# Attention and a rotating mixer: other ranks and a port rule for the opening, softmax sums beside a constant, first sine z's by two products, q and k behind vb

## The chip, the cores and the metric

The kernel runs on one core of a Trainium2 chip. The metric is the device time of one execution in microseconds; the time before is the median of three runs. The engines are called as in the profile: PE (TensorE), DVE (VectorE), ACT (ScalarE), POOL (GpSimd) and SP (SyncE, which issues the DMAs).

## The reference

```python
scores = q @ k.T / sqrt(64)                      # batch 8, heads 8, seq 576, head_dim 64
scores = where(mask, scores, -1e9)               # heads 0-3: last 32 keys; heads 4-7: every 4th of the last 128
attn = exp(scores - max);  attn = attn / (sum(attn) + 1e-9)
x = (attn @ v) as (8, 576, 512)
theta = x @ w_theta                              # 512 x 512
y = w_tok_r @ (x * cos(theta)) + w_tok_i @ (x * sin(theta))   # 576 x 576 each, over the sequence
u = x + y
out = u + relu(u @ w_ch)                         # 512 x 512, fp32 throughout
```

## The kernel before

The kernel works batch by batch, heads in four pairs (`pr`). Every large product is made in fp32 precision from rounded parts: an operand is split in a high part (a cast, on ACT) and a low part (the difference, on POOL), and three matmuls are added up. For the weights this split follows an unpacking: `unpack` clips (DVE, L407), scales (ACT, L409), prepares the second half (L412 on DVE or L415 on ACT) and joins the two (DVE, L417), and `split` makes the parts (ACT L425, POOL L427).

For each batch and pair: the scores `s` (PE, L547), their mask and maximum (DVE, L486, into P and mx), the exponential with the row sum (ACT, L582), the sum's reciprocal (L585 adds 1e-9, L586, both DVE), the normalisation of P (POOL, L588), the transposes pt<-P (DVE, L606) and the product with the values, `o` (PE, L702), which reads the values in two parts, `va` and `vb`. Then, for five row blocks `st` (4 is the short one), theta (`th`, L774 to L781), its sine and cosine (`trig`: K, f and g are scratch), x transposed (`xn`, L865) and its products with them, by_x (DVE, L856). These are the z's: z_0 to z_3 the cosine's, z_4 to z_7 the sine's, zh_8 and zl_8 both of the short block. `zsplit` makes their high part (a DVE cast, L730, in batch 0 for z_4 to z_8, otherwise ACT, L733) and their low part (POOL, L735). Token units `token(b, d, g)` compute y_d_g (PE, L1371), `residual` adds it to x (DVE, L1344) and splits u (ACT L1347, POOL L1349); channel units `chan(b, e, g)` compute c_e_g (PE, L1404), and `finish` does relu and add (DVE, L1380) and so frees their PSUM bank. In batch 0 all units take turns at the two banks "m". xh is x split for theta (L676 to L682).

From batch 2 on the token product is a faster scheme with sums of the token weights. These are built once, in batch 1, from wt_g, late_wt_a and others (POOL, L1069 to L1092), stored to DRAM (tw_t, tw_b; SP, L1098), and fetched in each batch (SP, L1049).

The order of the program on each engine is not written out by hand. The class `Order` runs the tasks as generators: each yields the engine that it wants next and an estimated cost in ns (functions dve, dve2, act, pool and others), or an event that it waits for, and of those ready on the engine that is free first the task of lowest rank goes. In the opening (batches 0 and 1) the ranks are the table RANK; after that `steady()` gives due times instead. What is pinned so is each engine's program order. Each engine, SP with its loads and stores too, works through its own order, and waits on the chip for whatever an instruction needs. Loads of q and k are in `load_qk` (L273, L275), of va and vb in L287 and L304.

Of the kernel before, what the change touches and what calls it, by code (L numbers as in the profile page):

```python
# [32 lines left out]
RANK = dict(load=6.64, scores0=1.09, flip=0.01, pv0=1.13, pair=.21, theta_unpack=1.54, theta0=5.3, trig0=2.41,  # L33
            token_early=2.55, theta_split=6.42, token_late=6.75, chan=2.1, units=2.95, evacuate=4.49,
            scores1=4.02, scores2=7.3, pv1=8.0, theta1=5.96, trig1=7.42)
# [45 lines left out]
class Order:  # L81
# [6 lines left out]
    def __init__(self, tc):  # L88
        self.tc = tc
        self.live = self.steady = False  # L90
        self.now = 0.0
        self.tasks, self.free, self.events = [], {}, {}
        self.serial = 0
        self.func = None

# [7 lines left out]
    def go(self, gen, rank=None):  # L103
# [5 lines left out]
        t = [self.rank if rank is None else rank, self.serial, self.now, gen, None, 0.0, None, False, 0.0]  # L109
# [3 lines left out]
    def advance(self, t):  # L113
        keep = getattr(self, "rank", None)
        self.rank = t[0]
        try:
# [12 lines left out]
            if t[7]:  # L129
                t[4] = "DVE"  # L130
# [6 lines left out]
    def run(self):  # L137
        while any(t[0] < BACK or self.steady for t in self.tasks):
# [7 lines left out]
            else:  # L146
# [9 lines left out]
                end = at + t[5]  # L156
                if eng == "ACT" and t[6]:
# [12 lines left out]
SLACK = 1500.0  # L170
# [15 lines left out]
def pool(n):  # L186
    return 2.36 * n
# [15 lines left out]
def build(ctx, tc, qT, kT, vw, wth, wtk, wch, maskb, ident, identb, outT):  # L203
# [60 lines left out]
    def load_qk(n):  # L264
# [4 lines left out]
        r = yield from take("qk", 2)  # L269
        q = ap.tile([128, 2 * NJ, 2 * QB], F32, tag="q", name=f"q{b}_{pr}")  # L270
# [20 lines left out]
    def load_vb(n):  # L291
# [51 lines left out]
    pqs, pts = [], []  # L343

# [41 lines left out]
    def unpack(src, sz, name, stage, early, n, key):  # L386
# [19 lines left out]
        yield "DVE", dve2(sz)  # L406
        pin(nc.vector.tensor_scalar(C, C, W_MAX, -W_MAX, op0=ALU.min, op1=ALU.max))  # L407
        yield "ACT", act(sz)
        pin(nc.scalar.activation(C, C, AF.Prelu, scale=2.0 ** -112, alpha=-2.0 ** 32))  # L409
        if early and n % 2 == 0:  # L410
            yield "DVE", dve2(sz)
            pin(nc.vector.tensor_scalar(Ti, Ti, 29, None, op0=ALU.logical_shift_right))  # L412
        else:
            yield "ACT", act(sz)
            pin(nc.scalar.activation(Ti, Ti, AF.Copy, scale=2.0 ** -29, bias=-0.5))  # L415
        yield "DVE", dve(sz)
# [101 lines left out]
    def scores(b, pr):  # L518
# [12 lines left out]
        sm = sp.tile([128, NJ], F32, tag=f"sm{b == 0 and pr}", name=f"sm{b}_{pr}", bufs=1 if b == 0 else 2)  # L531
# [39 lines left out]
        if b == 0:  # L571
# [3 lines left out]
            pin(nc.vector.tensor_reduce(sm, P, op=ALU.add, axis=mybir.AxisListType.X))  # L575
        elif not on_pe(b, pr):
            if b == 1:
                yield None, "sin0"
            for n0 in range(0, NJ, 3):
                yield "EXP", 1000 if od.steady else 720  # L580
                for n in range(n0, n0 + 3):
                    table(nc.scalar.activation(P[:, n], P[:, n], AF.Exp, bias=mx[:, n:n + 1], scale=-1.0,  # L582
                                               accum_out=sm[:, n:n + 1]))
        yield "DVE", 200
        pin(nc.vector.tensor_scalar(sm, sm, 1e-9, None, op0=ALU.add))  # L585
# [1073 lines left out]
```

## Time and profile before

| | |
|---|---|
| median of 3 runs | 564.25 us (562.17 to 565.25) |
| profiled execution | 563.72 us, of which the span 562.0 |
| PE busy | 532.8 us, 95% of the span |
| DVE busy | 440.9 us, 78% |
| ACT busy | 377.4 us, 67% |
| POOL busy | 332.4 us, 59% |

The span is the time from the first to the last instruction of the profiled execution; the rest of its 563.72 us lies around it. Busy shares are means over stages that differ: the opening, in which batch 0's attention and the unpacking of the weights share all engines, and the steady batches.

### The profile page before, as it was taken

Reading aid. Unit: us, or ns where it says so; the run is one execution under the profiler, and the core shown is the slowest. Engines: PE = TensorE matmul, PEld = TensorE weight load, DVE = VectorE, ACT = ScalarE, POOL = GpSimd, SP = SyncE. Lnnn points to the kernel's source line nnn. Section 1 sums busy time; section 2 is a strip of 40 time slices with the busy share of each in tenths; the row PEclk is TensorE's granted clock in tenths of the full one; section 3 lists DMA queues with packets and bytes.
Section 4 is the critical chain, followed back from the end, with each engine's and each line's share of the span. In section 5 each row is a group of like instructions: output and inputs, shape, how many; then the busy total and the mean of one; then the engine's idle time right before and its main releaser. Section 6 shows DMA issues by size and latency. Waiting matters only on the chain.

```text
span 562.0 us, 14370 instructions
## 1 busy us (share of the span) xinstructions
PE 532.8 (95%) x5296; PEld 483.3 (86%) x5296; DVE 440.9 (78%) x1347; ACT 377.4 (67%) x1033; POOL 332.4 (59%) x351
## 2 busy tenths in 40 slices
PE   5898798989999999999999999999999999999997
PEld 3644687868998899998999899989999899989997
DVE  3879698985579696999799997999799988838422
ACT  1598978768748577667876677768866777457320
POOL 1328759787994273674567284655468365817660
PEclk9999598989999999999999999999999999999999
DMA  8991436721678859985598919994798727690622
GB/s 299 400 390 28 178 117 217 250 81 65 207 244 276 298 213 310 317 247 202 175 351 275 302 54 338 320 244 152 257 342 235 269 91 235 188 265 24 224 93 86
DMA packets 59127, 124.42 MB, mean 221 GB/s; under 512 B 5424, under 2 KB 24624, under 8 KB 58800
## 3 DMA queue, kind: packets, MB, share of 16 engines
q1 hardware_dynamic: 59056, 123.49, 65.2%
q8 instruction: 42, 0.69, 0.5%
q14 instruction: 29, 0.24, 0.1%
HBM read 99.88 MB, written 23.59 MB: 220 GB/s over the span
## 4 chain that ended last, share of the span: by engine, by line
PE 58%; DVE 15%; POOL 8%; ACT 8%; DMA 7%; issue 3%; SPq 1%; POOLq 0%; DVEq 0%; ACTq 0%
PE c L1404 14%; PE th L774 11%; PE C L1167 7%; PE D L1167 6%; PE A L1167 4%; PE s L547 4%; PE B L1167 4%; PE o L702 3%; DVE pt L606 3%; DMA vb<-in_vw_dram 3%; PE y L1371 2%; ACT P L582 2%; DMA xn<-xd 1%; DVE st_wtk L417 1%; DMA first_k<-in_kT_dram 1%
## 5 line engine op out<-in xcount | busy, mean ns | idle before, releaser
L606 DVE STREAM_TRANSPOSE pt<-P 32x288 f32<-32x288 f32 x224 | 105.1, 469 | 13.0 <-POOL P L588 8.7
L1404 PE MATMUL c<-u,late_wc 128*128 128x288 f32 x768 | 108.5, 296 | 2.6 <-DVE x L1380 2.6
L1404 PEld LDWEIGHTS c<-u,late_wc 128*128 128x128 f32 x768 | 105.5, 188 | 5.4 <-DVE x L1380 2.8
L582 ACT ACTIVATE P<-P,mx 128x64 f32<-128x64 f32 x252 | 84.4, 336 | 8.3 <-DVE mx L486 8.1
L774 PE MATMUL th<-wthh,xh 128*128 128x512 f32 x224 | 75.9, 400 | 0.0
L588 POOL TENSOR_TENSOR P<-P,sm 128x576 f32<-128x576 f32 x32 | 37.4, 1168 | 60.7 <-DVE sm L586 53.5
L486 DVE CUSTOM_DVE_ANT_0 P<-s,mskb 128x64 f32<-128x64 f32 x252 | 38.7, 218 | 16.8 <-PE s L547 16.7
L774 PEld LDWEIGHTS th<-wthh,xh 128*128 128x128 f32 x224 | 42.9, 192 | 9.3
L1185 POOL TENSOR_TENSOR u<-x,u 128x288 fp32r<-128x288 f32 x48 | 38.5, 807 | 17.7 <-ACT u L1183 17.4
L1183 ACT CAST u<-x 128x288 fp32r<-128x288 f32 x48 | 20.4, 432 | 40.9 <-DVE x L1193 40.5
L582 ACT ACTIVATION_READ_ACCUMULATOR P<-P,mx 128x1 f32 x252 | 47.2, 187 | 0.0
L774 PE MATMUL th<-wthl,xh 128*128 128x512 f32 x112 | 45.0, 402 | 0.0
L662 ACT COPY x<-o 128x576 f32<-128x576 f32 x32 | 29.6, 924 | 18.6 <-PE o L702 18.5
L735 POOL TENSOR_TENSOR zl<-g,zh 128x512 fp32r<-128x512 f32 x7 | 9.1, 1295 | 54.8 <-ACT zh L733 46.1
L1380 DVE SCALAR_TENSOR_TENSOR x<-c,x 128x288 f32<-128x288 f32 x64 | 28.5, 452 | 13.3 <-PE c L1404 13.1
L547 PE MATMUL s<-k,q 128*64 128x64 f32 x1008 | 37.3, 229 | 0.8 <-PE y L1371 0.4
L547 PEld LDWEIGHTS s<-k,q 128*64 128x64 f32 x1008 | 33.6, 143 | 4.5 <-issue 2.6
L702 PEld LDWEIGHTS o<-pt,va 128*64 128x64 f32 x600 | 20.6, 137 | 9.3 <-issue 4.4
L702 PE MATMUL o<-pt,va 128*64 128x64 f32 x600 | 25.0, 227 | 3.7 <-DVE pt L606 2.2
L1371 PE MATMUL y<-wt_g,z 128*128 128x288 f32 x96 | 21.5, 329 | 4.9 <-POOL z L735 3.2
L947 POOL TENSOR_TENSOR s<-f,x 128x256 f32<-128x256 f32 x24 | 17.8, 741 | 12.7 <-DVE f L935 10.5
L774 PEld LDWEIGHTS th<-wthl,xh 128*128 128x128 f32 x112 | 21.3, 190 | 4.1
(241 smaller groups left out, 1596.6 us busy)
## 6 DMA issues: line engine op xcount, KB each, us to landing
q<-in_qT_dram SPq DMA_DIRECT2D x32, 576.0 KB, 5.5
late_wt_a<-tw_t SPq DMA_DIRECT2D x24, 576.0 KB, 5.7
wt_g<-tw_b SPq DMA_DIRECT2D x22, 576.0 KB, 6.4
va<-in_vw_dram SPq DMA_DIRECT2D x30, 320.0 KB, 5.0
k<-in_kT_dram SPq DMA_DIRECT2D x28, 304.0 KB, 6.3
out_dram<-x SPq DMA_DIRECT2D x28, 288.0 KB, 2.1
vb<-in_vw_dram SPq DMA_DIRECT2D x29, 256.0 KB, 4.3
xd<-xq SPq DMA_DIRECT2D x24, 288.0 KB, 4.9
```

Of the source, the lines that this page charges most:

```text
L486: pin(nc.vector.tensor_tensor_reduce(out=P[:, n], in0=ps[:, n - g0], in1=mskb[:, mask_of(pr, n)], op0=ALU.add, op1=ALU.min, scale=-SCALE, ...
L547: pe(nc.tensor.matmul(ps[64 * e:64 * e + 64, n - g0], q[:, qb], k[:, QB * qb:QB * qb + BW], start=not masked, stop=not masked or n == g1 - 1))
L582: table(nc.scalar.activation(P[:, n], P[:, n], AF.Exp, bias=mx[:, n:n + 1], scale=-1.0, accum_out=sm[:, n:n + 1]))
L588: pin(nc.gpsimd.tensor_tensor(P, P, sm.unsqueeze(2).to_broadcast([128, NJ, BW]), op=ALU.mult))
L606: pin(nc.vector.transpose(pmats[b, pr][k0:k0 + QB, :, hh, QB * e:QB * e + QB], P[p0:p0 + QB, :, QB * o:QB * o + QB]))
L662: pin(nc.scalar.copy(dst, src))
L702: pe(nc.tensor.matmul(ps[64 * hh:64 * hh + 64, BW * j:BW * j + BW], v[:, 64 * hh:64 * hh + 64], pmats[b, pr][:, j, hh], start=True, stop=T ...
L774: pe(nc.tensor.matmul(pt, l, r, start=(n == 0), stop=(n == 3 * NC - 1)))
L1167: pe(nc.tensor.matmul(ps, l, r, start=first and n == 1, stop=last and n == 3 * len(ks), skip_group_check=more))
L1185: pin(nc.gpsimd.tensor_tensor(ul[b, d][:, ts], x[:, ts], uh[b, d][:, ts].bitcast(F32), op=ALU.subtract))
L1371: pe(nc.tensor.matmul(ps, l[:, cs], r, start=(n == 0), stop=(n == 3 * NK - 1)))
L1404: pe(nc.tensor.matmul(ps, l[:, cs], r[:, ts], start=(n == 0), stop=(n == 3 * NC - 1)))
```

## The change

Four parts. First, other numbers: RANK (pair, trig0, token_late, trig1), SLACK, the costs of pool, of some ACT operations and of PE in the opening; and a rule, `port`, by which the planner in the opening lets operations of POOL and the DVE operations marked "DVE2" not overlap. Second, `sums`: four tiles of 9 x 2 values a partition, the second of each two set to 1e-9 once; the exponential adds its row sum into the first, and a reduction over the two replaces the addition of the constant; sum and reciprocal go to mx. Third, in batch 0 the high part of z_4 to z_7 is a second product of x and the sine, written rounded, instead of a copy of the first. Fourth, in the steady batches q and k of pairs 0 and 1 wait until vb of the next pair has its buffer, and so stand behind it on SP.

```diff
-RANK = dict(... pair=.21, ... trig0=2.41, ... token_late=6.75, ... trig1=7.42)
+RANK = dict(... pair=0.36, ... trig0=2.031, ... token_late=5.835, ... trig1=8.298)
...
+                if not self.steady and (t[9] or eng == "POOL"):
+                    end = max(at, self.port.get("POOL" if t[9] else "DVE", 0.0)) + t[5]
+                    self.port[eng] = end
...
-SLACK = 1500.0
+SLACK = 500.0
...
-    return 2.36 * n
+    return 80 + 2.31 * n
+def actf(n):
+    return 100 + 0.92 * n
...
+        if od.steady and b > FIRST and pr < 2:
+            yield None, ("vbi", b - 1, pr + 1)
...
             r = yield from take("vb", 1)
+            signal(("vbi", b, pr))
...
+    sums = [cp.tile([128, NJ, 2], F32, name=f"sums{n}") for n in range(NP)]
...
+        for t in sums:
+            pin(nc.vector.memset(t[:, :, 1], 1e-9))
...
-        yield "DVE", dve2(sz)
+        yield "DVE2", dve2(sz)
         pin(nc.vector.tensor_scalar(C, C, W_MAX, -W_MAX, op0=ALU.min, op1=ALU.max))
...
+        sm = sums[pr if b == 0 else pr % 2]
...
-                                               scale=SCALE, accum_out=sm[:, g0 + n:g0 + n + 1]))
+                                               scale=SCALE, accum_out=sm[:, g0 + n, :1]))
...
-        yield "DVE", 200
-        pin(nc.vector.tensor_scalar(sm, sm, 1e-9, None, op0=ALU.add))
-        pin(nc.vector.reciprocal(sm, sm))
+        yield "DVE", 300
+        pin(nc.vector.tensor_reduce(mx, sm, op=ALU.add, axis=mybir.AxisListType.X))
+        pin(nc.vector.reciprocal(mx, mx))
         yield "POOL", 1110
-        pin(nc.gpsimd.tensor_tensor(P, P, sm.unsqueeze(2).to_broadcast([128, NJ, BW]), op=ALU.mult))
+        pin(nc.gpsimd.tensor_tensor(P, P, mx.unsqueeze(2).to_broadcast([128, NJ, BW]), op=ALU.mult))
...
+        elif b == 0 and kt >= NC:
+            hi, lo = his[kt][:, :DM], his[kt][:, DM:]
...
-        if b == 0 and kt >= NC:
-            yield "DVE", dve2(DM)
+        if b == 0 and NC <= kt < 8:
+            pass
+        elif b == 0 and kt >= NC:
+            yield "DVE2", dve2(DM)
             pin(nc.vector.tensor_copy(hi, z))
...
-        yield "PE", 430
+        yield "PE", 640
...
+            if b == 0:
+                his[4 + st] = z_tile(f"z{b}_{4 + st}")
+                yield "DVE", dve(DM)
+                by_x(b, st, his[4 + st][:, :DM], sn)
             yield "DVE", dve(DM)
             by_x(b, st, g, sn)
...
```

What that does to the order is seen at three places. In the rows the name left of the arrow is written, those right of it are read; the last number of a name tells tiles apart, wtkl and wthl are low parts of token and theta weights, and the line numbers of the changed kernel are some 15 to 25 higher.

The first place is POOL at the first z's of batch 0. Before:

```order
L427 TENSOR_TENSOR wt_g<-st_wtk_1_185,wt_g 128x576
L735 TENSOR_TENSOR z_4_571<-Kg_0_537,z_4_571 128x512
L735 TENSOR_TENSOR zl_8_576<-Kg_4_518,zh_8_575 128x512
L427 TENSOR_TENSOR wtkl_565<-st_wtk_2_229,wtkh_564 128x576
L735 TENSOR_TENSOR z_0_605<-Kg_0_537,z_0_605 128x512
L735 TENSOR_TENSOR z_5_637<-Kg_1_591,z_5_637 128x512
```

And in the changed kernel, at the same place:

```order
L442 TENSOR_TENSOR wt_g<-st_wtk_1_190,wt_g 128x576
L442 TENSOR_TENSOR wtkl_545<-st_wtk_2_233,wtkh_544 128x576
L442 TENSOR_TENSOR wtkl_567<-st_wtk_3_346,wtkh_566 128x576
L754 TENSOR_TENSOR z_4_570<-Kg_0_532,z_4_570 128x512
L754 TENSOR_TENSOR zl_8_613<-Kg_4_526,zh_8_612 128x512
L754 TENSOR_TENSOR z_0_618<-Kg_0_532,z_0_618 128x512
```

Two splits of token weights now stand ahead of z_4. Three clips of token weights (L407) on DVE, which stood among z_5 to z_7, have gone behind the last z of batch 0, z_3.

The second place is the end of batch 0, first on PE: y_3_1 is the last token unit, th_4 batch 1's first theta. Before:

```order
L1371 MATMUL y_3_1_1397<-late_wt_b,zl_8_576 128x288
L1404 MATMUL c_0_0_1462<-u_0_813,late_wc_1167 128x288 x3
L779 MATMUL th_4_1454<-wthh_623,xh_0_1109 128x512
L781 MATMUL th_4_1454<-wthl_624,xh_0_1109 64x512
L778 MATMUL th_4_1454<-wthl_645,xh_1_1107 64x512
L779 MATMUL th_4_1454<-wthh_644,xh_1_1107 128x512
```

In the changed kernel:

```order
L1396 MATMUL y_3_1_1310<-late_wt_b,zl_8_612 128x288
L1429 MATMUL c_0_0_1407<-u_0_817,late_wc_1160 128x288 x3
L562 MATMUL s_1_5_1400<-k_1_1029,q_1_1028 64x64 x8
L1429 MATMUL c_0_0_1407<-u_1_868,late_wc_1203 128x288 x3
...
L1429 MATMUL c_2_0_1486<-u_0_817,late_wc_1160 128x288 x3
...
L1429 MATMUL c_3_0_1509<-u_3_1092,late_wc_1383 128x288 x3
L798 MATMUL th_4_1525<-wthh_594,xh_0_1110 128x512
```

The eight matmuls of th_4, and xn_4 behind them, have moved behind the 48 matmuls of c_0_0 to c_3_0. On DVE, around the relu-and-add of c_0_0 (x_0<-c_0_0), before:

```order
L606 STREAM_TRANSPOSE pt_110<-P_1_1274 32x9x32 x2
L1302 TENSOR_TENSOR g_4_1480<-th_4_1454,g_4_1480 64x512
L606 STREAM_TRANSPOSE pt_110<-P_1_1274 32x9x32 x2
L1380 SCALAR_TENSOR_TENSOR x_0_275<-c_0_0_1462,x_0_275 128x288
L1307 SCALAR_TENSOR_TENSOR K_4_1479<-g_4_1480,K_4_1479 64x512
```

And in the changed kernel:

```order
L621 STREAM_TRANSPOSE pt_116<-P_0_1190 32x9x32 x2
L1405 SCALAR_TENSOR_TENSOR x_0_279<-c_0_0_1407,x_0_279 128x288
L621 STREAM_TRANSPOSE pt_116<-P_0_1190 32x9x32 x2
L695 TENSOR_TENSOR xh_2_1330<-x_2_1188,xh_2_1330 128x64
L1405 SCALAR_TENSOR_TENSOR x_1_355<-c_1_0_1455,x_1_355 128x288
L621 STREAM_TRANSPOSE pt_116<-P_0_1190 32x9x32 x2
```

Before, four of the transposes of pair 1's P (P_1) and all eight of pair 0's (P_0) precede that relu-and-add; now four of pair 0's do. Eight transposes, xh_2 and the add of th_4 (g_4) now follow it.

The third place is SP in the first steady batch. Before:

```order
L273 DMA q_0_2769<-in_qT_dram 128x1152
L275 DMA k_0_2770<-in_kT_dram 128x608
L1049 DMA wt_g<-tw_t_1470 128x1152
L304 DMA vb_1_2829<-in_vw_dram 128x512
L287 DMA va_2_2828<-in_vw_dram 128x640
L273 DMA q_1_2854<-in_qT_dram 128x1152
L275 DMA k_1_2855<-in_kT_dram 128x608
L1049 DMA wt_g<-tw_t_1470 128x1152
L304 DMA vb_2_2959<-in_vw_dram 128x512
```

In the changed kernel:

```order
L1068 DMA wt_g<-tw_t_1466 128x1152
L316 DMA vb_1_2817<-in_vw_dram 128x512
L298 DMA va_2_2816<-in_vw_dram 128x640
L284 DMA q_0_2818<-in_qT_dram 128x1152
L286 DMA k_0_2819<-in_kT_dram 128x608
L1068 DMA wt_g<-tw_t_1466 128x1152
L316 DMA vb_2_2947<-in_vw_dram 128x512
L298 DMA va_3_2946<-in_vw_dram 128x640
L284 DMA q_1_2948<-in_qT_dram 128x1152
```

q and k of pairs 0 and 1 follow vb and va now, instead of standing ahead of them. Earlier on the same queue, in batch 1, vb of pair 3 of batch 2 stood ahead of the stores tw_t<-td and tw_t<-ta, the last of the sums; now it stands behind these two, and five stores of tx that were ahead of it follow it. On POOL one operation on tx has likewise gone behind the last one on ta.

More of the change, by code (lines that the diff above doesn't have):

```diff
@@ L94, in __init__ @@
         self.func = None
+        self.port = {}
     def pin(self, ins):
@@ L660, in x_evac @@
             src = src.rearrange("p (c j) -> p c j", c=4)
-        yield "ACT", 580
+        yield "ACT", 580 if od.steady or pr < NP // 2 else 970
         pin(nc.scalar.copy(dst, src))
@@ L766, in theta @@
         n = 0
-        yield "PE", (231 if od.steady else 215) * (12 if st < 4 else 8)
+        yield "PE", 231 * (12 if st < 4 else 8)
         for c in range(NC):
```

37 lines of the change are left out of this document (19 added, 18 removed).

## The prediction

> **What bounds the kernel now.** I read the busy time by stretch first, because the share over the whole span hides where TensorE waits. Each row gives the stretch and its length, then busy us of PE, PEld, DVE, ACT and POOL, then the clock granted to TensorE (1.00 is full), the share of DMA and GB/s.
>
> ```profile
> 57.00:70.40 13.40, 10.22 (x66) 9.11 (x67) 8.31 (x39) 12.50 (x46) 10.85 (x9) 0.50 0.45 162
> 66.00:125.00 59.00, 53.01 (x532) 47.44 (x533) 51.54 (x164) 45.18 (x145) 46.12 (x45) 0.90 0.48 158
> 94.50:98.00 3.50, 3.50 (x37) 2.99 (x34) 3.46 (x6) 2.64 (x5) 3.38 (x4) 0.51 0.59 173
> 121.90:125.30 3.40, 3.40 (x9) 2.64 (x8) 3.25 (x7) 1.98 (x3) 3.29 (x4) 0.51 0.00 0
> 125.30:170.00 44.70, 44.70 (x469) 41.98 (x468) 27.08 (x87) 30.63 (x83) 39.56 (x45) 1.00 0.51 167
> 170.00:562.00 392.00, 384.48 (x3690) 361.00 (x3689) 313.92 (x977) 258.47 (x725) 217.12 (x236) 1.00 0.69 228
> ```
>
> From 170 us on PE is busy 384.48 of 392.00 us: little is to be had there. In 66 to 125 it is busy 53.01 of 59, so 6.0 us are idle, while VectorE works 51.54 of 59: VectorE is the tighter engine there. Half speed costs as well: in 57 to 70.4 PE ran at 0.50 of its clock for 10.22 busy us, and in 94.5 to 98 and 121.9 to 125.3 at 0.51 for 6.9. At full speed these 17.1 us of work would take half, 8.6. Next, what PE waited for up to 165 us (total, times, longest):
>
> ```profile
> PE s L547 <- DMA first_k<-in_kT_dram: 3.6, 2, 3.4
> PE y L1371 <- POOL z L735: 3.2, 3, 1.5
> PE o L702 <- DVE pt L606: 2.2, 2, 1.2
> PE y L1371 <- ACT z L733: 1.6, 1, 1.6
> ```
>
> The token units y wait 4.8 us for the first z's (3.2 for GpSimd's low halves, 1.6 for ScalarE's high half), and o waits 2.2 for transposes of the probabilities; the one wait of the channel units stands below. The 3.6 for the first keys are loads and untouched. What the change can win in the opening is these waits and some of the half-speed time.
>
> **Part 1, order of the first z's (ranks, port rule, costs).** The last of batch 0's z's is z_3. ScalarE rounds it, GpSimd forms its low half, and PE's y resumes:
>
> ```profile
> ACT wtkh L425 <- DVE st_wtk L417: 1.5, 1, 1.5
> ACT g L1314 <- DVE K L1307: 0.7, 1, 0.7
> ACT st_wtk L409 <- DVE st_wtk L407: 0.5, 1, 0.5
> ...
> 63.97 0.60 ACT L733 CAST z<-K 128x512 fp32r<-128x512 f32 x1
> 64.65 1.26 POOL L735 TENSOR_TENSOR z<-K,z 128x512 fp32r<-128x512 f32 x1 [0.76 <-ACT z L733]
> 65.97 0.61 PE L1371 MATMUL y<-wt_g,z 128*128 128x288 f32 x1 [0.50 <-POOL z L735]
> ```
>
> Up to that cast ScalarE has the same instructions in both orders, but for one 576-wide clip that goes and one 576-wide copy that comes. Of its waits, 1.5 + 0.7 + 0.5 = 2.7 us in 33 to 66, the 1.5 for VectorE is now filled, because the cast that waited (wtkh of the short block) stands later on ScalarE, and three of VectorE's clips of token weights are put behind z_3. I leave 0.6 of waiting: z_3 comes 2.7 - 0.6 = 2.1 us earlier, and y with it. Bounds: 0 (a new wait of equal size, since z_4 now stands behind two splits on GpSimd) to 2.7. I take 2.1 because the waits that go are rows, and the one that might come is short of a row. **Term A: -2.1.**
>
> **Part 2, the end of batch 0.** Here PE waits at c_2_0 for the bank that the relu-and-add of c_0_0 frees:
>
> ```profile
> 73.69 3.87 DVE L606 STREAM_TRANSPOSE pt<-P 32x288 f32<-32x288 f32 x8
> ...
> 112.57 0.37 DVE L680 TENSOR_TENSOR xh<-x,xh 128x64 fp32r<-128x64 f32 x1
> 113.94 0.69 DVE L682 TENSOR_TENSOR xh<-x,xh 128x512 fp32r<-128x512 f32 x1
> 118.95 0.68 DVE L1302 TENSOR_TENSOR g<-th,g 64x512 f32<-64x512 f32 x1
> 120.65 0.46 DVE L1380 SCALAR_TENSOR_TENSOR x<-c,x 128x288 f32<-128x288 f32 x1
> ...
> 113.64 0.39 PE L778 MATMUL th<-wthl,xh 128*64 128x512 f32 x1
> 113.87 0.39 PE L779 MATMUL th<-wthh,xh 128*128 128x512 f32 x1
> 115.62 0.60 PE L865 MATMUL xn<-ids,x 128*64 128x128 f32 x4
> 121.17 0.67 PE L1404 MATMUL c<-u,late_wc 128*128 128x288 f32 x3 [2.57 <-DVE x L1380]
> ```
>
> In the new order eight transposes (3.87, as the row of eight has it), both halves of xh_2 (0.37 + 0.69) and theta_4's add (0.68) stand behind that relu-and-add: 5.6 us less ahead of it. The add's time is then 120.65 - 2.1 - 5.6 = 112.95, and c_2_0 goes on 0.52 later (121.17 - 120.65), at 113.5: 7.7 us sooner. But PE has moved too: the eight matmuls of th_4 and the four of xn_4 that it had done by then now come after the channel units. Eight at 0.23 from start to start (113.64 to 113.87) are 1.8, and xn_4 0.60: 2.4 still owed. PE is ahead by 7.7 - 2.4 = 5.3, in which A is contained; **term B is 5.3 - 2.1 = -3.2.** From PE's side: it stood 2.57 at that place, and 2.57 + 2.1 = 4.7; its 2.2 us of waits for transposes may go as well, 6.9 at most. 5.3 lies between 4.7 and 6.9, so I keep it. Lower bound of B: 0, if the work that VectorE puts off meets the trigonometry of batch 1 (rival 1). Upper, for A and B together: all of the 6.0 idle, and half of the 6.9 us at half speed (3.4), which is 9.4 (rival 4).
>
> What is late next? At 173 us PE waits for vb of pair 3, the second part of its values. SyncE's queue is in order, and vb stands in it behind stores of the weight sums that GpSimd computes.
>
> ```profile
> PE o L702 <- DMA vb<-in_vw_dram: 2.4, 4, 1.2
> 167.11 0.81 POOL L1092 TENSOR_TENSOR tb<-tb,tc 128x288 fp32r<-128x288 f32 x1
> 167.87 0.82 POOL L1092 TENSOR_TENSOR ta<-ta,td 128x288 fp32r<-128x288 f32 x1
> 168.49 2.12 SPq L304 DMA_DIRECT2D vb<-in_vw_dram  x1
> ```
>
> The first row is PE's wait for vb from 160 to 520: 2.4 us, four times, the longest 1.2, which is this place. Before, GpSimd's tb (167.11 to 167.92) released the last store ahead of vb, which went out at 168.49. Now the store of ta stands ahead of it as well, one operation later on GpSimd, 167.87 - 167.11 = +0.76; but five stores of tx and one operation of tx on GpSimd have gone behind, -0.76 by the same spacing: 0. What costs is that GpSimd must be as far ahead as PE: PE waits there already, so every microsecond that GpSimd lags behind PE's 5.3 is paid. GpSimd works 46.12 of 59 us and then 39.56 of 44.70, so it has 12.9 + 5.1 = 18.0 of idle time from which to shed 5.3. **Term D: +1.0**; bounds 0 (it sheds all 5.3) and +5.3 (none, rival 2). I take the low end because 5.3 is under a third of 18.0, and not 0 because part of that idle time is waiting for other engines.
>
> **Part 3, q and k behind vb.** In the steady batches vb's transfer no longer follows the q and k of pairs 0 and 1. The three other waits make 2.4 - 1.2 = 1.2 us. I take half, since the wait is also set by the bank of values that frees late. **Term C: -0.6**, bounds 0 and -1.2. Queued behind the new wait are q and k themselves, and the scores wait for them:
>
> ```profile
> 278.27 1.13 SPq L287 DMA_DIRECT2D va<-in_vw_dram  x1
> 285.49 0.42 SPq L287 DMA_DIRECT2D va<-in_vw_dram  x1
> 290.16 1.22 PE L547 MATMUL s<-k,q 128*64 128x64 f32 x36
> 299.78 1.22 PE L547 MATMUL s<-k,q 128*64 128x64 f32 x36
> q<-in_qT_dram SPq DMA_DIRECT2D x32, 576.0 KB, 5.5
> ```
>
> These are, of the batch that begins at 275 us, two issues of va (SyncE), the scores of pairs 0 and 1 (PE), and from the page q's landing time, 5.5. Behind va at 278.27 + 1.13 the transfer lands at about 279.5 + 5.5 = 285.0, and is used at 290.16; behind the second, at 285.9 + 5.5 = 291.4, used at 299.78. Covers of 5 and 8 us hide it. If they were gone, PE would wait up to the 5.5 of a transfer in each pair; neither row comes near that, so 0.
>
> **Part 4, edits costed at nothing.** Durations by form (smallest, median, largest ns):
>
> ```profile
> L730 DVE CAST z<-Kg x2: 407/594/781, 44.0 to 50.3; 128x512 fp32r<-128x512 f32 x2
> L730 DVE CAST z<-g x2: 414/728/1043, 55.7 to 60.8; 128x512 fp32r<-128x512 f32 x2
> L856 DVE TENSOR_TENSOR Kg<-xn,Kg x6: 676/684/692, 40.6 to 51.9; 128x512 f32<-128x512 f32 x4, 64x512 f32<-64x512 f32 x2
> L585 DVE TENSOR_SCALAR sm<-sm x32: 129/174/785, 13.0 to 470.6; 128x9 f32<-128x9 f32 x32
> L735 POOL TENSOR_TENSOR z<-K,z x6: 1265/1290/1323, 59.3 to 145.7; 128x512 fp32r<-128x512 f32 x6
> L735 POOL TENSOR_TENSOR z<-Kg,z x4: 1405/1462/1485, 44.5 to 53.9; 128x512 fp32r<-128x512 f32 x4
> ```
>
> The casts of z_4 to z_7 were 0.407 + 0.781 + 0.414 + 1.043 = 2.65 us; four products at 0.683 to 0.684 are 2.73, so +0.1 on VectorE, and it stands where VectorE's other work was put off. What changes is GpSimd: its four low halves from Kg took a median of 1.462 against 1.290 from K, 4 x 0.17 = 0.7 us together. I count none of it, for what PE waits for last is ScalarE's z_3 and the low half behind it; were it all on the path, -0.7. Row then rule: a cast took 0.41 alone and 1.04 beside GpSimd, the product 0.68 in every place. The Trainium skill, "SBUF — State Buffer", section "SBUF: two separate sides", says that an operation of VectorE in a two-port mode and one of GpSimd lock each other out for the whole instruction, while an operation with one SBUF input outside those modes does not take the pair; the product reads one operand from PSUM. By that rule the 0.7 us on GpSimd are won, and the sum would be up to 0.7 lower; the traces agree with it for the casts, and none here shows the new product into a rounded tile.
>
> The softmax sums: 32 additions of a constant (median 0.174) become reductions over twice as many elements. No row has that form; between the smallest and twice the median, 0.13 to 0.35, four of them on VectorE's path in 66 to 125 make -0.2 to +0.7; taken 0, as the reciprocal behind each is unchanged and 0.17 is the row for the same small tile. The four memsets at the start, at 0.13 each at most 0.5 us, lie under PE's 3.6 us for the first keys. The costs and SLACK are numbers of the planner; they change order only.
>
> **Sum.** The profiled execution took 563.72 (span 562.0); the median of the runs is 564.25, 0.5 above. 563.7 - 2.1 - 3.2 - 0.6 + 1.0 = 558.8; on the scale of the median **559.3**.
>
> **Rivals.** (1) The opening gains only z_3. VectorE's work is put off, not removed: transposes of pairs 0 and 1 then stand between the channel adds and batch 1's trigonometry, and PE meets there what it shed before. For it: 51.54 of 59. Against: VectorE works only 27.08 of 44.70 us afterwards. Then, with D at 0 because GpSimd need be only 2.1 ahead, 563.7 - 2.1 - 0.6 = 561.0, or 561.5 by the median.
>
> (2) No change: GpSimd or SyncE takes the gain back at vb. Everything that PE gained is waited for there: 563.7 - 0.6 = 563.1, or 563.6. For it: GpSimd's 39.56 of 44.70, and the 1.2 that PE waits already. Against: its 12.9 us idle before.
>
> (3) Slower: PE parks at the channel units. With 48 matmuls of c in a row ahead of th_4, PE has nothing else to do while it waits for the banks. The point that decides is the relu-and-add of c_0_0: past 120.65 - 2.4 = 118.25 PE is behind. If that add comes at 120.65 as before, PE stands there 2.57 + 2.4 = 5.0 us and still owes the 2.4; I add two more stretches of 3.4 us at half speed, 1.7 lost in each, and take off the 1.2 of vb, which is then there in time: 563.7 + 2.4 + 3.4 - 1.2 - 0.6 = 567.7, or 568.2. For it: PE lost its clock at every such stand. Against: eight transposes less ahead of the add. The Trainium skill, "TensorE: Matmul & The Clock Gate", Part 1, says the clock is judged over free-running windows of about 3.4 us, and that an idle one halves it; by that rule a stand of 5.0 us speaks against the change; the rows at 94.5 (3.50 us at 0.51) and 121.9 (3.40) agree with it in length.
>
> (4) Much faster: PE sheds the 6.0 idle and 3.4 of half speed, and vb keeps pace: 563.7 - 9.4 - 0.6 = 553.7, or 554.2. VectorE's 51.54 less 5.6 in 59 would allow it; against it speak the 2.2 us for transposes, which come from the same VectorE.
>
> **How the numbers follow.** Forecast 0.46 (own range 556 to 561.4), rival 1 0.18, rival 2 0.13, rival 3 0.11, rival 4 0.12. The bound of a change that can be told is 0.5%, 2.8 us: 561.4 to 567.1. Rival 1 lies on the lower one, so half of it counts as faster: 0.46 + 0.12 + 0.09 = 0.67; same 0.09 + 0.13 = 0.22; slower 0.11. The range from 554.0 to 564.5 leaves out rival 3 and, of rival 4, the half that would come out under 554: 0.17.
>
> **What would show it.** A: the wait of y for ScalarE's and GpSimd's z together under 3 us, y's resumption near 64 instead of 65.97. B: the relu-and-add of c_0_0 near 113, the wait there under 1 us, th_4 after it. D: PE's wait for vb at about 168, near 2. C: the later waits for vb together near 0.6. It is wrong if the stretch to 125 us has no less than 6 us idle, or if vb's first wait grows by as much as PE was ahead.

## The result and the profile after

The changed kernel takes 558.77 us (median of 10 runs, 556.04 to 562.91) against 563.29 (10 runs, 560.71 to 565.25): a ratio of 0.9918 with an interval of 0.9894 to 0.9941, some 4.6 us. The profiled execution took 557.11 us with a span of 555.3, a little faster than the median, as that of before (563.72) was a little slower; so the traces differ by 6.6 us, 2 more than the medians.

The same stretches as in the prediction (us, then busy us of PE, PEld, DVE, ACT and POOL, granted clock, DMA, GB/s):

```profile
57.00:70.40 13.40, 10.15 (x86) 9.15 (x86) 11.95 (x49) 13.38 (x49) 11.76 (x10) 0.87 0.46 158
66.00:125.00 59.00, 54.79 (x573) 49.94 (x571) 52.62 (x169) 43.61 (x138) 46.94 (x47) 0.97 0.50 163
94.50:98.00 3.50, 3.50 (x65) 3.04 (x67) 3.47 (x16) 2.10 (x3) 2.17 (x3) 1.00 0.77 250
121.90:125.30 3.40, 3.05 (x16) 2.40 (x14) 3.03 (x6) 3.30 (x5) 2.87 (x4) 1.00 0.23 87
125.30:170.00 44.70, 41.82 (x485) 38.20 (x487) 29.59 (x102) 32.34 (x91) 38.65 (x43) 1.00 0.53 173
170.00:555.00 385.00, 381.05 (x3631) 357.92 (x3627) 304.72 (x958) 254.69 (x717) 217.29 (x235) 1.00 0.69 231
```

From 66 to 125 us PE is now busy 54.79 of 59 (53.01 before) and VectorE 52.62 (51.54): VectorE was no less full, but further. The stretches at half speed near 96 and 123 us are gone. PE's waits up to 165 us:

```profile
PE o L717 <- DVE pt L621: 3.7, 2, 2.3
PE y L1396 <- POOL z L754: 2.5, 3, 1.3
PE y L1396 <- ACT z L752: 2.4, 1, 2.4
```

The wait of the channel units for the relu-and-add, 2.57 before, is not in the list. Of y's waits 1.28 stand in batch 1 (shown below), so for batch 0's first z's it waited 3.6 in all, against 4.8 before; o waits longer for transposes (3.7 against 2.2). The chain from z_3 (GpSimd's low half, then y on PE), then the relu-and-add of c_0_0 on VectorE, then the channel units and the first theta on PE:

```profile
63.25 1.34 POOL L754 TENSOR_TENSOR z<-K,z 128x512 fp32r<-128x512 f32 x1 [0.41 <-ACT z L752]
64.64 0.40 PE L1396 MATMUL y<-wt_g,z 128*128 128x288 f32 x1 [0.88 <-POOL z L754]
...
112.64 0.46 DVE L1405 SCALAR_TENSOR_TENSOR x<-c,x 128x288 f32<-128x288 f32 x1
...
111.29 5.37 PE L1429 MATMUL c<-u,late_wc 128*128 128x288 f32 x37 [0.21 <-POOL late_wc L442]
116.50 0.39 PE L798 MATMUL th<-wthh,xh 128*128 128x512 f32 x1
```

y resumes at 64.64 instead of 65.97, the relu-and-add stands at 112.64 instead of 120.65, and the 37 matmuls of c run without a wait from 111.29 on. The next fence has the first scores of batch 2 on PE, before and after: the two programs have done the same matmuls there.

```profile
145.47 1.27 PE L547 MATMUL s<-k,q 128*64 128x64 f32 x36
...
139.76 1.27 PE L562 MATMUL s<-k,q 128*64 128x64 f32 x36
```

So 5.71 us were won by then in these two traces. Two waits of the changed kernel follow, and the first row of the scores behind vb's old place:

```profile
145.50 0.40 PE L1396 MATMUL y<-wt_g,z 128*128 128x288 f32 x1 [1.28 <-POOL z L754]
168.30 0.80 PE L717 MATMUL o<-pt,va 128*64 128x64 f32 x20 [0.97 <-ACT x L677]
169.40 1.22 PE L562 MATMUL s<-k,q 128*64 128x64 f32 x36
```

At y of batch 1 PE waits 1.28 for GpSimd's z_3. At 168.30 it waits 0.97 for ScalarE to empty the bank of o, and vb, which cost 1.16 before, is there in time (in e2, without part 4, PE waits 0.43 for it here). These scores stood at 173.58 before, so 4.18 are left. The rest of the 6.7 comes in the steady batches (1.7) and at the last batch's first step (0.8).

### The profile page after: what moved, and what is told of

Read it like the earlier page. It is cut to its first block, busy times and chain, and to the rows that moved or that the text cites. A ratio compares the mean times of both kernels' runs of the same rounds, so it can differ in the third digit from the quotient of the medians.

```text
span 555.3 us, 14353 instructions
## 1 busy us (share of the span) xinstructions
PE 529.5 (95%) x5296; PEld 479.5 (86%) x5296; DVE 434.9 (78%) x1351; ACT 375.2 (68%) x1033; POOL 333.1 (60%) x351
## 4 chain that ended last, share of the span: by engine, by line
PE 69%; DVE 9%; ACT 8%; POOL 6%; DMA 5%; issue 2%; SPq 1%; POOLq 0%; ACTq 0%; DVEq 0%
PE c L1429 14%; PE th L793 11%; PE C L1186 8%; PE A L1186 7%; PE D L1186 6%; PE o L717 5%; PE s L562 5%; PE B L1186 4%; PE y L1396 4%; DVE pt L621 3%; PE th L775 2%; DMA xn<-xd 1%; DMA first_k<-in_kT_dram 1%; POOL z L754 1%; DMA st_wch<-in_wch_dram 1%
## 5 line engine op out<-in xcount | busy, mean ns | idle before, releaser
L603 POOL TENSOR_TENSOR P<-P,mx 128x576 f32<-128x576 f32 x32 | 38.3, 1196 | 60.5 <-DVE mx L601 51.5
L1204 POOL TENSOR_TENSOR u<-x,u 128x288 fp32r<-128x288 f32 x48 | 41.7, 875 | 14.4 <-ACT u L1202 14.0
L562 PE MATMUL s<-k,q 128*64 128x64 f32 x1008 | 36.1, 224 | 1.9 <-DVE K L1328 1.7
L562 PEld LDWEIGHTS s<-k,q 128*64 128x64 f32 x1008 | 32.3, 138 | 5.7 <-issue 2.1
```

The lines of the kernel that those rows point to most:

```text
L562: pe(nc.tensor.matmul(ps[64 * e:64 * e + 64, n - g0], q[:, qb], k[:, QB * qb:QB * qb + BW], start=not masked, stop=not masked or n == g1 - 1))
L603: pin(nc.gpsimd.tensor_tensor(P, P, mx.unsqueeze(2).to_broadcast([128, NJ, BW]), op=ALU.mult))
L1204: pin(nc.gpsimd.tensor_tensor(ul[b, d][:, ts], x[:, ts], uh[b, d][:, ts].bitcast(F32), op=ALU.subtract))
```

## The experiments

All twelve kernels were timed in five rounds beside the kernel before, in four sets; its medians there were 562.55 to 563.25. A ratio need not be the quotient of two medians, and the change itself was timed in a set of its own, so that it is compared with the runs by the ratios to before.

| run | what it is | median us | ratio to before | interval |
|---|---|---|---|---|
| | the change | 558.77 | 0.9918 | 0.9894 to 0.9941 |
| e1_vb_only | before + part 4 | 563.44 | 1.0004 | 0.9980 to 1.0027 |
| e2_no_vb | change without part 4 | 559.08 | 0.9941 | 0.9918 to 0.9963 |
| e3_old_ranks | change without part 1 | 565.12 | 1.0043 | 1.0025 to 1.0060 |
| e4_no_sums | change without part 2 | 560.73 | 0.9970 | 0.9950 to 0.9989 |
| e5_sums_only | before + part 2 | 562.84 | 0.9992 | 0.9966 to 1.0019 |
| e6_no_port | change without the port rule | 567.72 | 1.0088 | 1.0051 to 1.0125 |
| e7_casts | change without part 3 | 567.65 | 1.0088 | 1.0056 to 1.0121 |
| e8_other_bank | before, c_0_0 in another bank | 567.24 | 1.0059 | 1.0033 to 1.0085 |
| e9_copy_same_order | change, copies in the products' places | 559.73 | 0.9939 | 0.9905 to 0.9972 |
| e10_transposes_first | change, old end of batch 0 | 560.34 | 0.9943 | 0.9914 to 0.9972 |
| e11_order_only | before + part 1 | 564.32 | 1.0017 | 0.9992 to 1.0042 |
| e12_clip_with_sum | change, clips with an accumulator | 558.98 | 0.9910 | 0.9878 to 0.9942 |

### Part 4: q and k behind vb

e1 puts the rule into the kernel before, e2 takes it out of the changed one:

```diff
 r = yield from take("qk", 2)
+if od.steady and b > FIRST and pr < 2:
+    yield None, ("vbi", b - 1, pr + 1)
```

> The kernel before with the fourth part alone (q and k of pairs 0 and 1 behind vb in the steady batches); PE's order is as before in every row. The traces of before and after differ by 4.18 us at the scores behind 173 us, 4.13 one batch later, and then 4.77, 5.24 and 5.84 in the next batches, so part 4 should be worth the 1.7 us that are added there. Theory: 563.3 - 1.7 = 561.6, the three later waits of PE for vb (1.2 us together before) gone, the first one at 172 us (1.2) still there. Rival 1, the size that was forecast: -0.6, 562.7, half of the waits left. Rival 2, the steady gain belongs to the shifted opening and not to part 4: 563.3, waits as before.

> The changed kernel without its fourth part; PE's order as in the changed kernel in every row. Theory: 558.8 + 1.7 = 560.5, with waits for vb in the three later batches again (0.3 to 0.5 each), the opening as in the changed kernel (relu-and-add of c_0_0 near 112.6, first scores of batch 2 near 139.8). Rival 1: 559.4. Rival 2: 558.8 with no waits for vb.

PE's waits for vb from 155 to 520 us, first in e1, then in e2:

```profile
PE o L705 <- DMA vb<-in_vw_dram: 1.6, 1, 1.6
```

```profile
PE o L715 <- DMA vb<-in_vw_dram: 1.0, 2, 0.6
```

In e1 the three later waits are gone and the first is left (1.6 in this execution); in e2 vb costs 1.0 in two waits, where the changed kernel has none. Between the same scores one batch behind the opening and four batches later (211.43 and 458.75 before) the traces take 247.32 before and 246.15 with part 4, 246.57 in e2 and 245.66 with it: 1.2 and 0.9 us. But other executions differ by as much there. Without part 4 the same stretch took 246.14 in e5, 246.27 in e8 and 245.72 in e11; with it 245.58 to 246.16 in e4, e6, e7, e9, e10 and e12, but 247.79 in e3. PE's waits for vb from 205 to 475 us were 1.2, 0.6, 0.3, 0.3 and 0 in the five traces without part 4 (before, e2, e5, e8, e11), and 0 in seven of the nine with it (0.3 in e7, 0.8 in e3). So with part 4 these waits are mostly gone, but not only there and not always, and whether it is worth 1 us, the forecast 0.6 or less can't be told; the 1.7 of these expectations, read off one pair of traces, is not borne out. The times cannot show 1 us either: e1's interval reaches down to 0.9980, which is 1.1 us, and e2's overlaps that of the change.

### Part 1: the planned order

e3 undoes ranks, SLACK, costs and the port rule, e11 adds these alone to the kernel before, and e6 takes only the port rule out:

```diff
-if not self.steady and (t[9] or eng == "POOL"):
+if False:
```

> The changed kernel with its first part undone: old ranks, slack, costs, no port rule; sums, second products and the vb rule stay. Here th_4 stands ahead of c_2_0 on PE again and the relu-and-add of c_0_0 behind ten to twelve transposes. Theory (part 1 carries the opening's gain): the wait at c_2_0 is back with 2 us or more, the first scores of batch 2 come within 2 us of 145.5, and the time is 563.3 - 1.7 = 561.6. Rival (the products and sums carry it, by freeing GpSimd and VectorE): relu-and-add of c_0_0 before 116, time 558 to 559.5.

> The changed kernel without the port rule of the planner; ranks and costs of the change stay. th_4 then stands ahead of c_2_0 on PE again, as before. Theory (the rule is what puts c_0_0 to c_3_0 ahead of th_4 and the transposes behind the relu-and-add): most of part 1's gain is lost, a wait at c_2_0 of 2 us or more, first scores of batch 2 near 145, 562 to 564. Rival (the ranks and costs carry it): 558.5 to 560, no wait there.

> The kernel before with part 1 alone (ranks, slack, costs, port rule); c_0_0 to c_3_0 stand ahead of th_4 as in the changed kernel, z_4 to z_7 are casts, the sums as before, q and k ahead of vb. Theory (part 1 carries the gain, the others add to it): ratio 0.994 to 0.998, 560 to 561.8. Rival (the numbers of part 1 fit only the instructions of parts 2 and 3 together, as the run without the products and the run with old ranks, both slower than before, suggest): ratio 1.003 or more, 564 to 568, with the loss in batch 1's theta, 125 to 170 us, as in the run without the products.

e3 is slower than before, 1.0043, by more than the theory had: part 1 is worth 1.2% to the other three, and these lose without it. The wait at c_2_0 that the theory named is not back; PE waits 1.00 for VectorE earlier in the channel units (118.22). In e6 the planner puts th_4 ahead of c_2_0 again. The rows are the relu-and-add of c_0_0 (VectorE) in e3, then in e6, and a wait of PE in e6:

```profile
121.13 0.46 DVE L1407 SCALAR_TENSOR_TENSOR x<-c,x 128x288 f32<-128x288 f32 x1
```

```profile
124.98 0.46 DVE L1405 SCALAR_TENSOR_TENSOR x<-c,x 128x288 f32<-128x288 f32 x1
...
135.09 0.63 PE L884 MATMUL xn<-ids,x 128*128 128x128 f32 x4 [2.13 <-DVE g L875]
```

Both adds are late. In e6 the wait stands not at c_2_0 but a step on, 2.13 for a product on VectorE: of what the expectation said, the time (567.7 against 562 to 564), the first scores (155.31 against 145) and the place were wrong, the side right. Without the port rule the ranks of the change do no better than those of before with the same other parts (1.0088 against 1.0043 in e3).

Part 1 alone (e11) won nothing. Its relu-and-add comes at 113.60, as in the changed kernel, and the gain is given back behind it. The rows are PE's in e11 at batch 1's third and fourth theta, then its first scores of batch 2:

```profile
135.27 0.50 PE L783 MATMUL th<-wthh,xh 128*128 128x512 f32 x1 [0.39 <-DVE K L1316]
139.96 0.50 PE L783 MATMUL th<-wthh,xh 128*128 128x512 f32 x1 [1.15 <-DVE K L1316]
143.42 1.27 PE L556 MATMUL s<-k,q 128*64 128x64 f32 x36
```

No channel unit is left between these two thetas: PE waits 0.39 and 1.15 for VectorE to free theta's bank, and the first scores stand at 143.42, 2.05 sooner than before (145.47) where the changed kernel has 5.71. The two waits are 1.5 of these 3.7; at the next scores e11 is behind the kernel before (153.44 against 151.55). In the changed kernel channel units (c, six or three matmuls) stand between all thetas up to 139.19 and fill these waits. The rival was right in kind, with 1.0017 under the 1.003 that it gave.

### Part 3: two products

e7 makes z_4 to z_7 by casts again and lets the planner order anew; e9 keeps every row of the order and writes a copy in the place of the second product:

```diff
-                by_x(b, st, his[4 + st][:, :DM], sn)
-            yield "DVE", dve(DM)
-            by_x(b, st, g, sn)
+                by_x(b, st, g, sn)
+                yield "DVE", dve(DM)
+                pin(nc.vector.tensor_copy(his[4 + st][:, :DM], g))
```

> The changed kernel without its third part: z_4 to z_7 by casts from SBUF again; the planner then orders the stretch around the first z's a little otherwise. Theory (the products are worth what the lock costs, 0.7 on GpSimd, and it lies partly on the path): 558.8 + 0 to 1.5; casts between 0.41 and 1.05 us, GpSimd's low halves beside them above 1.40, where the changed kernel has 1.27 to 1.34. Rival (the products only add work, 0.68 against 0.41): 558 or less.

> The changed kernel in which, in batch 0, the sine z is made first and the high part of z_4 to z_7 is a VectorE copy of it, in the two places where the changed kernel has its two products: the orders of all engines are those of the changed kernel but for these eight rows on VectorE. It measures the product against the copy by itself. Theory (the copy is short alone, 0.41, and up to 1.05 beside GpSimd, and disturbs GpSimd; z_4 to z_7 all come one operation earlier as values but later as high parts): 558.8 + 0 to 0.8, low halves of z_4 to z_7 on GpSimd above 1.40 in two to four of four, resumption of y after z_3 within 0.7 of 64.6. Rival (what the run without the products lost, 9 us, was the product's own): 562 or more.

e7 is 9 us slower than the change; e9, with the same copies, is not told apart from it (0.9939 against 0.9918, the intervals overlap). So the 9 us are the order's and not the product's. PE's wait for theta's bank in e7 up to 165 us, then two of its thetas of batch 1:

```profile
PE th L789 <- DVE K L1324: 2.5, 3, 1.2
...
139.67 0.50 PE L789 MATMUL th<-wthh,xh 128*128 128x512 f32 x1 [1.15 <-DVE K L1324]
144.35 0.51 PE L789 MATMUL th<-wthh,xh 128*128 128x512 f32 x1 [1.15 <-DVE K L1324]
```

Its channel units are used up at 129 us, and the thetas behind them wait, as in e11. The copies of e9 by form (smallest, median, largest ns), and y on PE behind z_3:

```profile
L1344 DVE CAST z<-Kg x2: 416/974/1531, 46.3 to 51.6; 128x512 fp32r<-128x512 f32 x2
L1344 DVE CAST z<-g x2: 515/668/820, 54.3 to 58.9; 128x512 fp32r<-128x512 f32 x2
...
64.34 0.40 PE L1399 MATMUL y<-wt_g,z 128*128 128x288 f32 x1 [1.28 <-POOL z L754]
```

A copy took 0.42 to 1.53 us, where the changed kernel's products into a rounded tile took 0.675 to 0.692, all four. y resumes at 64.34, against 64.64 with products, but this execution was ahead by then: the twelve matmuls of batch 0's theta that stand in a row began at 32.03, against 33.17. From there to y's resumption e9 takes 32.31, the changed kernel 31.47, and e2, e4 and e10, which have the products too, 31.44 to 31.46. So in this trace the copies cost 0.84 on that path, where the forecast had nothing (0.7 if all of it were on the path). GpSimd's low halves of z_4 to z_7 took 1.27 to 1.44 in both kernels, no longer beside the copies, against the expectation; but GpSimd waited for the copies, and the low half of z_3 took 1.74 instead of 1.34.

### Part 2: the softmax sums

e4 takes the sums out of the changed kernel, e5 adds them to the one before; the orders of PE and SyncE are the changed kernel's in e4, and those of before in e5.

```diff
-pin(nc.vector.tensor_reduce(mx, sm, op=ALU.add, axis=mybir.AxisListType.X))
-pin(nc.vector.reciprocal(mx, mx))
+pin(nc.vector.tensor_scalar(sm, sm, 1e-9, None, op0=ALU.add))
+pin(nc.vector.reciprocal(sm, sm))
```

> The changed kernel with the addition of 1e-9 by its own instruction as before; orders of PE and SyncE as in the changed kernel in every row. Theory (part 2 costs and wins nothing): 558.8, within 0.7 either way; the additions take 0.13 to 0.8 us, those beside GpSimd the long ones, where the reductions all took 0.16 to 0.17. Rival (the long additions lie on the path): 0.3 to 0.6 for each of two or three, 559.8 to 560.5.

> The kernel before with the softmax sums of the change alone (memsets, reduction over the constant); PE's and SyncE's orders are those of before in every row. Theory after the run without the sums (additions of 0.95 and 0.62 us beside GpSimd's splits there, reductions of 0.17 in their place): the additions beside GpSimd (0.43, 0.46 and 0.32 in 66 to 125 us before) shrink to 0.17, 0.7 us less on VectorE ahead of the relu-and-add of c_0_0: ratio 0.997 to 0.999, 561.5 to 562. All 32 reductions between 0.15 and 0.22. Rival (the 0.5% by which the run without sums fell short is another cause, as when loads came): 562.5, ratio 1.000.

The form of the 32 small operations in the changed kernel, then in e4, and after it three of e4's on VectorE and the wait of o on PE:

```profile
L600 DVE TENSOR_REDUCE mx<-sums x32: 129/165/174, 13.0 to 464.7; 128x9 f32<-128x18 f32 x32
```

```profile
L597 DVE TENSOR_SCALAR sm<-sm x32: 131/239/3272, 12.7 to 467.7; 128x9 f32<-128x9 f32 x32
...
83.74 0.95 DVE L597 TENSOR_SCALAR sm<-sm 128x9 f32<-128x9 f32 x1 [0.38 <-ACT P L594]
93.94 0.62 DVE L597 TENSOR_SCALAR sm<-sm 128x9 f32<-128x9 f32 x1
152.51 3.27 DVE L597 TENSOR_SCALAR sm<-sm 128x9 f32<-128x9 f32 x1
...
95.86 0.74 PE L714 MATMUL o<-pt,va 128*64 128x64 f32 x17 [3.67 <-DVE pt L618]
```

Beside GpSimd the addition of 128 x 9 numbers took 0.95, 0.62 and once 3.27 us; at 152.51 it stood while GpSimd, which had its operations back to back from 150.4 to 155.7, worked through four of them. The reduction, of twice as many numbers, never took more than 0.174. In the changed kernel the next operation of VectorE at that place waits instead, xh of 128 x 64, until GpSimd's first gap at 153.05:

```profile
150.52 2.61 DVE L695 TENSOR_TENSOR xh<-x,xh 128x64 fp32r<-128x64 f32 x1 [0.26 <-ACT xh L691]
```

The time agrees with a loss: 0.9970, with an interval that does not touch that of the change, 1 to 5 us. Where it is lost is less clear. In the changed kernel o waited 2.31 at 94.42, in e4 3.67 at 95.86, which is 1.44 later. The rows are VectorE's first clip of channel weights behind the addition, in the changed kernel, in e4 and in e10, an experiment below that has the reductions and the changed kernel's order up to there; then e10's wait of o:

```profile
87.38 0.91 DVE L422 TENSOR_SCALAR st_wch<-st_wch 128x512 f32<-128x512 f32 x1 [0.71 <-DMA st_wch<-in_wch_dram]
...
89.56 0.82 DVE L419 TENSOR_SCALAR st_wch<-st_wch 128x512 f32<-128x512 f32 x1 [2.32 <-DMA st_wch<-in_wch_dram]
...
90.02 0.58 DVE L422 TENSOR_SCALAR st_wch<-st_wch 128x512 f32<-128x512 f32 x1 [3.33 <-DMA st_wch<-in_wch_dram]
95.59 1.17 PE L717 MATMUL o<-pt,va 128*64 128x64 f32 x17 [3.38 <-DVE pt L621]
```

SyncE issued these loads at 83.0 to 83.1 in all three, ahead of the first long addition (83.74). Behind that addition VectorE stood idle for a load that landed later in e4 than in the changed kernel, so that its 0.78 beyond 0.17 cost nothing at o. The transposes ahead of the second stand 0.98 later (92.97 against 91.99); only the 0.45 of the second comes on top. And in e10, without any addition, o waited 3.38, because that load came later still. Before this place e4 lost 1.05 (from y behind z_3 to the scores at 79 us, 15.51 against 14.46): behind an addition of 0.30 a join of weights (L429) took 1.76 instead of 0.81. That the long additions are what e4 loses is thus argued, not shown. In the kernel before the same sums win nothing that can be told (e5, 0.9992), though all 32 shrank there as well. Why the same shorter operations win nothing there stays open.

### The end of batch 0 by itself

e8 puts c_0_0 (and c_3_0) in a third bank, x, in the kernel before, so that c_2_0 no longer waits for c_0_0; batch 1's xn uses that bank too; e10 makes the relu-and-add of c_0_0 wait for pair 0's transposes in the changed one, and the planner then puts th_4 ahead of c_2_0 as before the change.

```diff
-return "mmx"[n % 3] if b else "m"
+return "mmx"[n % 3] if b or n >= 2 * NC else "m"
```

```diff
 x = xf[b, e]
+if (b, e, g) == (0, 0, 0):
+    yield None, ("pt", 2, 0)
```

> The kernel before with batch 0's channel units on three banks (m, m, x) as batch 1 has them, so that c_2_0 need not wait for the relu-and-add of c_0_0; the order ahead of it is as before. It is to show what that one wait (2.57 us) is worth by itself. Theory (the wait is the price, and removing it alone gives 2 to 2.6, less where xn and the channel units now share a bank): 560 to 561.5. Rival (VectorE stays the bound and the wait only moves to the next bank): 562.5, ratio 1.000.

> The changed kernel in which the relu-and-add of c_0_0 has to come after the transposes of pair 0 of batch 2; the planner then puts th_4 and xn_4 ahead of c_2_0 on PE, as before the change. All engines' orders are those of the changed kernel up to that place. Theory (term B: that arrangement is where the 2.57 us stood): relu-and-add of c_0_0 near 116 to 117 instead of 112.6, PE waits 1 to 3 at c_2_0 or for what follows, first scores of batch 2 at 141 to 143 instead of 139.8, 560 to 562. Rival (the gain is made before that place, in the first z's and the rows around them, and the end of batch 0 only passes it on): 558.8, first scores within 0.7 of 139.8.

PE's waits in e8, and where the two long ones stand:

```profile
PE c L1404 <- DVE K L856: 2.4, 1, 2.4
PE xn L865 <- DVE x L1380: 2.0, 2, 1.8
...
119.93 0.63 PE L865 MATMUL xn<-ids,x 128*64 128x128 f32 x4 [1.85 <-DVE x L1380]
145.20 3.44 PE L1404 MATMUL c<-u,late_wc 128*128 128x288 f32 x24 [2.38 <-DVE K L856]
```

The 2.57 are gone from c_2_0. But xn_4 now stands behind c_0_0 in the bank x and waits 1.85 for the same relu-and-add, and 25 us later a channel unit waits 2.38 for the product that empties that bank. Both come from the shared bank, and the kernel is slower than before. So e8 shows that this exchange does not pay; what the one wait alone was worth, it can't show. In e10 (PE's channel units, the relu-and-add on VectorE, the first wait behind them, the first scores of batch 2):

```profile
113.07 1.98 PE L1431 MATMUL c<-u,late_wc 128*128 128x288 f32 x13 [0.21 <-POOL late_wc L442]
...
116.56 0.45 DVE L1407 SCALAR_TENSOR_TENSOR x<-c,x 128x288 f32<-128x288 f32 x1
...
126.64 1.09 PE L884 MATMUL xn<-ids,x 128*128 128x128 f32 x4 [2.58 <-DVE g L875]
144.52 1.27 PE L562 MATMUL s<-k,q 128*64 128x64 f32 x36
```

Up to the channel units, where the order is still the changed kernel's, this execution is 1.78 us later (113.07 against 111.29), by the late load shown above; at the first scores it is 4.76 later (144.52 against 139.76, where 141 to 143 was expected). So between the two the old arrangement costs 3.0 us in this pair of traces (31.45 against 28.47), and 2.1 against e4, which takes 29.39 with the new one (e9 28.50). That is near term B, forecast at 3.2. The time moves that way, 0.9943 against 0.9918, but does not prove it.

### A try to go on: clips that do not lock

```diff
-pin(nc.vector.tensor_scalar(C, C, W_MAX, -W_MAX, op0=ALU.min, op1=ALU.max))
+pin(nc.vector.tensor_scalar(C, C, W_MAX, -W_MAX, op0=ALU.min, op1=ALU.max, accum_out=clipped))
```

> The changed kernel in which the 18 clips of the weights (VectorE, 0.40 to 1.53 us there, median 0.46 for the token weights and 0.97 for the channel weights) also write an accumulator that nobody reads; all engines' orders are those of the changed kernel. The Trainium skill, SBUF — State Buffer, section Who interferes with whom, says that tensor_scalar enters the two-port mode that locks GpSimd out, but not in the form that also writes out its accumulator. Theory (by that rule the clips no longer wait for GpSimd, nor GpSimd for them): every clip takes the same 0.55 to 0.75 us, none above 0.8; VectorE loses some 0.2 on each short clip and wins 0.3 to 0.9 on each long one, and the time is 557.5 to 559.5 against 558.8. Rival (the accumulator form contends as well, or is simply longer): durations spread up to 1.5 as before, and 559.5 to 562.

The clips of the changed kernel, then those of e12, by form:

```profile
L422 DVE TENSOR_SCALAR st_wtk<-st_wtk x10: 402/456/1526, 33.0 to 67.2; 128x576 f32<-128x576 f32 x8, 128x288 f32<-128x288 f32 x2
L422 DVE TENSOR_SCALAR st_wch<-st_wch x4: 433/974/1375, 87.4 to 102.9; 128x512 f32<-128x512 f32 x4
```

```profile
L423 DVE TENSOR_SCALAR_CACHE_REDUCE st_wtk<-st_wtk x10: 444/742/753, 34.4 to 69.7; 128x576 f32<-128x576 f32 x8, 128x288 f32<-128x288 f32 x2
L423 DVE TENSOR_SCALAR_CACHE_REDUCE st_wch<-st_wch x4: 682/686/687, 90.6 to 105.3; 128x512 f32<-128x512 f32 x4
```

The rule of the expectation holds here: none of the clips of 512 or 576 is longer than 0.753, where the changed kernel has up to 1.53. Yet 0.9910 against 0.9918 is no difference: each clip beside an idle GpSimd now takes 0.69 or 0.74 instead of 0.42 or 0.46.

## Why the prediction was right, and where it was not

The time, 558.77 against 559.3, was right, and so was the main mechanism: VectorE's work goes behind the relu-and-add, and PE gains at the end of batch 0. That the total came so near is in part luck. The terms missed in both directions, as the list shows, and the traces differ by 2 us more than the medians. Of the signs, y's resumption (64.64), the add (112.64) and the idle time (4.2 us up to 125) came; the waits of y for z's (3.6, not under 3), the wait for vb at 168 (none, not 2) and the later waits for vb (none, not 0.6) did not.

- **Term A** (z_3, -2.1): y resumes 1.33 earlier (65.46 to 66.05 in the traces of before, e1, e5 and e8, 63.66 to 65.29 in those of the change, e2, e4 and e10). ScalarE's 1.5 for VectorE went, and its waits fell from 2.7 to 1.6, not to 0.6: a new one of 1.1 stands at a clip of the theta weights. The step "I leave 0.6 of waiting" was too small.
- **Term B** (A and B together -5.3, the add at 112.95): 5.71 at the first scores, the add at 112.64. e10 gives 2.1 to 3.0 for the rearranged end of batch 0 by itself, which bears out the mechanism in the traces. That 5.71 met 5.3 is luck too: it holds what the sums were worth, which the prediction put at nothing (without them, in e4, the first scores stood at 142.45, 2.7 later, part of it that execution's late load).
- **Term D** (+1.0 at vb): the amount came, 1.5 between 139.76 and 169.40, but not at vb. It stands at y of batch 1, 1.28 for GpSimd's z_3, and 0.97 at o's bank, for ScalarE; less the 1.16 that went at vb, 1.1 of the 1.5. GpSimd lagged, as the term said; I had looked only at the wait that the trace of before showed.
- **Term C** (-0.6): 0.9 to 1.2 in the two pairs of traces, all three waits; but executions of one kind differ by more, and neither half nor all is shown.
- **Part 4, edits at nothing:** the products were worth 0.8 on the path to y in the trace of e9, where the prediction had 0 and at most 0.7; the times don't tell it from nothing. The sums were worth 1 to 5 by the times, and were put at 0 with +0.7 to -0.2. The step that failed there was "0.17 is the row for the same small tile": I took the median of L585 and let its largest, 0.785, stand in the same row unread. That the length of the additions is all of the loss is not shown. The Trainium skill, "SBUF — State Buffer", section "Who interferes with whom", says that tensor_scalar can enter the mode that locks against GpSimd and that tensor_reduce on trn2 never does; I used that page for the casts alone. These runs agree with it, 0.95 and 3.27 against 0.17.
- **Half speed:** I counted 8.6 us of lost work as something that could be won. In e5, PE's order is that of before, and the clock in 57 to 70.4 was 0.87 instead of 0.50; y on PE behind z_3, and that stretch:

```profile
64.55 0.53 PE L1374 MATMUL y<-wt_g,z 128*128 128x288 f32 x2 [3.21 <-ACT z L736]
65.89 0.61 PE L1374 MATMUL y<-wt_g,z 128*128 128x288 f32 x1 [0.82 <-POOL z L738]
...
57.00:70.40 13.40, 8.11 (x72) 7.21 (x73) 8.76 (x39) 12.58 (x47) 10.85 (x9) 0.87 0.47 164
```

y resumes at 65.89 against 65.97. Faster matmuls only waited longer for z (3.21 against 1.63 before the first, 0.82 against 0.50): half speed cost nothing there. In e5 the clock was 1.00 at 94.5 to 98 and 121.9 to 125.3 too, and the sums were shorter; yet the first scores came only 0.69 sooner than before (144.78). Rival 4 counted 3.4 for these two stretches.

Rival 1 did not come in the changed kernel, yet e7 and e11 show it: the same end of batch 0, and the gain lost at batch 1's theta. That the changed kernel escapes it hangs on the order that the planner makes of parts 1 and 3 together (e9, with copies in that order, keeps the gain), which the sum of separate terms could not tell: part 1 gives +0.2% alone and -1.2% beside the others.

## What to carry to other kernels

A list scheduler's rule and the instructions that it plans have to be judged together: e7 and e11 have the same early relu-and-add as the change and lose it one stage later, since the fillers between two waits were spent. Before a wait for a bank is taken away by another bank, ask who uses that one: the wait of 2.57 came back as 1.85 and 2.38. Where a small operation of VectorE stands beside GpSimd, read its largest duration too, not its median alone. And before a wait in a trace is put down to an edit, look for the same wait in a run without that edit: o's 3.67 in e4 stood as 3.38 in e10, for a late load.

## What the runs showed of the hardware

An addition of 9 numbers a partition stood 3.27 us on VectorE while GpSimd went from one operation to the next: the one that waits is not served after the first operation of the other. In the changed kernel xh, 128 x 64, stood 2.61 in the same way, until a gap in GpSimd's operations. Clips of 512 or 576 numbers with an accumulator took 0.67 to 0.75 us wherever they stood, those without 0.40 to 1.53.
